# A new order of 1382 hand-ordered steps in a fused DeltaNet and feed-forward kernel

## The chip, the cores and the metric

The kernel runs on one core of one Trainium2 chip. The metric is the device time of one execution in microseconds (us). The engines have the profile's names: PE is TensorE (PEld is its loading of weights), DVE VectorE, ACT ScalarE, POOL GpSimd, and SP the engine that issues most of the DMA transfers.

## The reference

Inputs q, k, v have the shape 4 x 8 x 768 x 48 (batch, heads, tokens, features), beta 4 x 8 x 768. For each batch and head a state of 48 x 48 is carried over the tokens; the outputs of all heads side by side are a matrix x of 3072 x 384, which goes through a feed-forward block.

```python
k_n = k / (norm(k) + 1e-6)
for t in range(768):
    y[t] = q[t] @ state
    v_old = k_n[t] @ state
    state = state + beta[t] * outer(k_n[t], v[t] - v_old)
x = y as (3072, 384)                   # one row per token, heads side by side
out = (((x @ w1) * (x @ w2)) @ w3) @ w_out   # w1, w2: 384 x 1024, w3: 1024 x 1024, w_out: 1024 x 384
```

## The kernel before

The tokens are cut into 12 chunks of 64. Within a chunk the recurrence is solved as a whole: the scores of keys against keys form a strictly lower triangular matrix, its inverse is formed by elimination, and a few small products then give the outputs and the next state. Two chunks make a unit (512 tokens of all batches); each unit's outputs go through the feed-forward block, so there are six units, u = 0 to 5. The two last weights are multiplied once ahead (w3 @ w_out, the "fold"), after w3 has been transposed on PE.

Every part of the work is a Python generator, named by a letter and a number. `ORDER` (L39) is a text of 1382 names: `step` (L1320) advances the named generator to its next `yield`, which issues the instructions of one step, and `in_text_order` (L186) makes each engine keep the order in which its instructions were issued. Across engines only data and buffers order the work. The text is thus the queue of every engine, SP's and POOL's among them. The names:

- Loads on SP: k, q, v (chunks of the inputs), p (keys and queries of later chunks in another layout), P (pieces of the weights: load L838, a copy on ACT L846, a shift on DVE L851 and a sum on POOL L853 that rewrite the piece).
- K, Q (L369 on PE; 64 small products and copies on ACT L379 and DVE L381) and d (DVE) bring keys and queries into the layout of features. g and N make norms: squares on POOL (L301), sums on DVE (L303), and N's fifteen short operations on DVE.
- s (scores; s0 and s1 have 128 products at L409 and U on DVE at L420; the later ones L451, L457 with U and PT on DVE at L463, L474), h (scores of the first queries, L400, with PT on DVE at L434), u (U to memory, Ud, on SP).
- V (L497), one for each unit: the inverses by elimination. V0 takes U from on chip by a transpose on DVE (L505), V1 to V5 load Ub from Ud (SP, L510). Then 31 steps of two DVE operations each (L524, L529), each needing the one before. V0 and V1 eliminate in PSUM. V0 ends with four transposes on DVE (L533), the others with a store (SP, L549).
- e (L597): the corners that join two blocks of 32 into an inverse of 64: loads from Vd or, for e0 and e1, products on PE (L563); a transpose on DVE (T11, L602); products c1 and c2 on PE (L619) with copies on ACT.
- n scales v (POOL, L658). c (L664) is the chain from chunk to chunk: R, X and the state S, each one set of 64 products on PE (L672) and one DVE operation (L706, L717, L738). y (L744) gives the outputs: products on PE (L777), xT by ACT and SP.
- t (L900) transposes a part of w3, f (L910) folds: two halves of eight products (L913) and a copy on ACT.
- The feed-forward block: b (the first chunk of unit 0) and a0 to a4 are the products with w1 and w2 (`ab`, L927: six products at L934 and a copy on ACT, six more and a multiplication on DVE, L950), a50 to a53 those of unit 5 in another scheme (L1055). S, T, W and X are the sums on POOL and DVE that a Strassen-like scheme needs. o (L1143) is the product with the folded weight: seven steps of 16 products (L1166), and x (L1193) adds its parts (osb on ACT and DVE, L1197) and stores the result (SP).

PSUM is used as four banks (`ps_f`: a, b, t, f, o, K, Q, norms) and two pairs of banks (`ps_w`: scores, corners, chain, outputs, and V0 and V1 while they eliminate).

A step with large products lasts 2.6 us on PE (o, a, a half of f), a step with 64 or fewer small ones, of 32 to 64 columns, mostly less than 1 us. The order was written out in full; nothing in the file computes it.

Of the kernel before, what the change touches and what calls it, by code (L numbers as in the profile page):

```python
# [57 lines left out]
p5 c2 c2 e3 c2 x0 S0 o0 c3 S0 e3 c3 o0 e3 N2 y2 c3 x0 o0 d4 p5 y2 S0 c3 y3 x0 x0 x0 d5 d5 s4 s4
o0 x0 y3 s4 s4 d5 d5 s4 s4 N2 s5 y3 u4 s5 V2 s5 s5 s5 N2 s5 c3 u5 V2 x0 p6 x0 a14 p6 a14 a14 a14
a13 a13 V2 V2 V2 V2 V2 a12 a12 V2 a16 a16 V2 V2 V2 V2 V2 V2 V2 a15 V2 a15 a11 a11 V2 V2 V2 V2 V2  # L60
V2 V2 V2 V2 v5 x0 V2 a10 V2 V2 k6 V2 v4 V2 V2 V2 V2 a17 a17 a15 a15 a10 k7 d6 d6 d6 a10 a10 c3
S1 n5 n4 a13 a12 a12 a13 V2 e4 a17 e4 a11 g3 g3 g3 g3 a11 Q3 c4 g3 g3 n4 c4 e4 a16 a16 e5 e4 e4
e4 o1 x1 S1 a17 S1 S1 S1 e5 e5 S1 e5 d6 n5 g3 c4 c4 g3 o1 S1 c4 V3 c4 g3 e5 e5 o1 p7 g3 N3 c5 p7
# [6 lines left out]
S2 S2 d9 d9 p10 S2 e7 c7 S2 x2 o2 d9 d9 c7 S2 s8 c7 x2 s8 o2 s8 c7 S2 y7 S2 v8 n8 x2 K1 o2 x2 x2  # L70
u8 Q2 s9 s9 S2 S2 s9 y7 y7 s9 s9 u9 S2 o2 x2 s9 c7 x2 c7 V4 a32 a32 N4 k10 x2 x2 a36 a36 d10 d10
V4 a30 a30 V4 V4 a33 a35 Q1 V4 a37 V4 V4 V4 V4 a33 V4 V4 c8 V4 V4 V4 V4 a35 a37 V4 V4 V4 k11 a34
n9 a34 a31 p10 V4 V4 V4 V4 a34 V4 V4 V4 V4 x2 V4 V4 V4 V4 V4 V4 V4 e8 a31 d10 a31 a31 a35 a34 V5
a33 a30 a30 a36 n8 c8 K3 e8 e8 a35 a37 a33 a36 e8 K3 e8 e8 a37 a32 e9 e9 e9 p11 e9 c8 a32 o3 x3
S3 S3 g5 g5 g5 g5 n9 g5 S3 c8 d10 S3 S3 S3 c8 e9 p11 g5 g5 g5 o3 o3 e9 c8 c9 x3 x3 S3 S3 g5 g5
# [1283 lines left out]
```

## Time and profile before

| | before |
|---|---|
| time, median of 3 runs | 556.95 us (556.87 to 558.0) |
| the profiled execution: span | 556.1 us |
| its own time | not listed apart; the span is 0.85 us below the median of the runs |
| PE busy, instructions | 533.6 us (96%), 8732 |
| DVE busy, instructions | 343.7 us (62%), 800 |
| ACT busy | 145.7 us (26%) |
| POOL busy | 169.7 us (31%) |
| moved by DMA | 54.22 MB |
| instruction queue q8 | 68 packets, 1.11 MB |

By stages (start and end in us, PE busy, DVE busy, share of the DMA engines' time):

| stage | window | PE | DVE | DMA |
|---|---|---|---|---|
| loads, first scores | 0 to 32 | 20.41 | 23.40 | 0.92 |
| fold, V0, first chain | 32 to 100 | 66.58 | 51.04 | 0.82 |
| b and a0, V1 | 100 to 146 | 45.67 | 32.42 | 0.64 |
| o0 and the small steps of chunks 2 to 5 | 146 to 183 | 35.36 | 21.94 | 0.34 |
| a1, V2 | 183 to 227 | 44.00 | 32.04 | 0.61 |
| o1 and small steps | 227 to 265 | 36.27 | 22.58 | 0.47 |
| a2, V3 | 265 to 311 | 46.00 | 36.71 | 0.61 |
| o2 and small steps | 311 to 342 | 30.77 | 11.78 | 0.40 |
| a3, V4 | 342 to 388 | 46.00 | 32.26 | 0.44 |
| o3 and small steps | 388 to 420 | 31.59 | 17.86 | 0.26 |
| a4, V5 | 420 to 465 | 45.00 | 29.37 | 0.40 |
| o4 and small steps | 465 to 496 | 29.37 | 7.17 | 0.08 |
| a5 | 496 to 534 | 38.00 | 16.04 | 0.04 |
| o5, last results | 534 to 556.1 | 18.55 | 9.08 | 0.11 |

How to read it: the span is from the first to the last instruction of the profiled execution. Busy time of PE is counted from modelled ends of pipelined products. The granted clock of PE is 1.00 in every stage. A releaser named "issue" means that the engine waited for nothing that the profile shows.

### The profile page before, as it was taken

How to read it: one execution, taken by the hardware profiler on the slowest of the kernel's cores; microseconds unless marked ns; L12 is line 12 of the kernel's file. 1: busy time of each engine (PE TensorE's matmuls, PEld its weight loads, DVE VectorE, ACT ScalarE, POOL GpSimd, SP SyncE). 2: the span in 40 equal slices, each digit the busy share in tenths (PEclk: the TensorE clock that was granted, in tenths of full speed). 3: DMA queues.
4: the chain of work that ended last, by engine and by line, in shares of the span. 5: the costliest groups of instructions: out<-in, count | busy, mean ns of one | idle time of the engine just before them, and what ended most of it. 6: DMA issues, size and time to landing. Idle time of an engine off the chain costs nothing.

```text
span 556.1 us, 19932 instructions
## 1 busy us (share of the span) xinstructions
PE 533.6 (96%) x8732; PEld 390.8 (70%) x8732; DVE 343.7 (62%) x800; ACT 145.7 (26%) x291; POOL 169.7 (31%) x213
## 2 busy tenths in 40 slices
...
GB/s 189 339 307 230 158 140 150 128 160 55 96 48 55 119 147 72 67 88 89 122 74 100 70 91 80 126 38 83 51 15 154 26 60 38 18 58 1 0 2 57
DMA packets 191527, 54.22 MB, mean 98 GB/s; under 512 B 178928, under 2 KB 185072, under 8 KB 191440
## 3 DMA queue, kind: packets, MB, share of 16 engines
...
q8 instruction: 68, 1.11, 0.9%
...
## 4 chain that ended last, share of the span: by engine, by line
PE 93%; DVE 3%; issue 2%; DMA 2%; ACT 0%; SPq 0%; DVEq 0%
PE ps_f L934 38%; PE ps_f L1166 20%; PE ps_f L913 7%; PE ps_w L672 6%; PE ps_w L777 4%; PE ps_f L1074 4%; PE ps_w L619 3%; PE ps_w L1074 2%; PE ps_w L451 2%; PE ps_f L369 1%; PE ps_w L457 1%; PE ps_f L904 1%; DMA beta_fm<-in_beta_dram 1%; PE ps_w L409 1%; PE ps_w L1166 1%
## 5 line engine op out<-in xcount | busy, mean ns | idle before, releaser
L934 PE MATMUL ps_f<-xT,w2s 128*128 128x512 f32 (+1 forms) x288 | 106.9, 524 | 0.0
L934 PE MATMUL ps_f<-xT,w1s 128*128 128x512 f32 (+1 forms) x288 | 106.7, 524 | 0.0
L934 PEld LDWEIGHTS ps_f<-xT,w2s 128*128 128x128 f32 x288 | 54.1, 190 | 46.5 <-issue 41.6
L934 PEld LDWEIGHTS ps_f<-xT,w1s 128*128 128x128 f32 x288 | 54.0, 190 | 45.3 <-issue 41.6
L1007 POOL TENSOR_TENSOR ab<-ab 128x256 f32<-128x256 f32 x80 | 56.4, 731 | 78.7 <-DVE ab L950 73.8
L946 ACT COPY ab<-ps_f 128x512 f32<-128x512 f32 (+1 forms) x48 | 24.3, 515 | 134.4 <-PE ps_f L934 130.3
L1166 PE MATMUL ps_f<-w,ab 128*128 128x192 f32 x320 | 57.3, 332 | 1.9 <-DVE osb L1197 1.3
L1166 PEld LDWEIGHTS ps_f<-w,ab 128*128 128x128 f32 x320 | 51.6, 190 | 3.3 <-issue 2.4
L524 DVE TENSOR_TENSOR tb<-Vb,Ub 128x31 f32<-128x31 f32 (+15 forms) x124 | 43.0, 347 | 15.4 <-DMA Ub<-Ud 11.5
L529 DVE TENSOR_TENSOR Vb<-Vb,tb 128x31 f32<-128x31 f32 (+15 forms) x124 | 43.0, 346 | 4.3
L913 PE MATMUL ps_f<-wo,w3T 128*128 128x384 f32 x128 | 43.5, 491 | 0.4 <-ACT w3T L907 0.4
L1166 PE MATMUL ps_f<-room,ab 128*128 128x192 f32 x240 | 42.8, 332 | 0.0
L950 DVE TENSOR_TENSOR ab<-ab,ps_f 128x512 f32<-128x512 f32 (+1 forms) x48 | 27.4, 589 | 24.0 <-PE ps_f L934 24.0
L1166 PEld LDWEIGHTS ps_f<-room,ab 128*128 128x128 f32 x240 | 38.7, 190 | 0.7
L913 PEld LDWEIGHTS ps_f<-wo,w3T 128*128 128x128 f32 x128 | 23.5, 190 | 15.4 <-ACT w3T L907 0.5
L301 POOL TENSOR_TENSOR sq<-ktok 128x384 f32<-128x384 f32 x24 | 19.7, 835 | 43.5 <-DMA out_dram<-osb 16.9
L658 POOL TENSOR_TENSOR vtok<-vtok,n 128x384 f32<-128x384 f32 x24 | 19.8, 832 | 39.5 <-DMA vtok<-in_v_dram 39.5
L635 ACT COPY T<-ps_w 32x512 f32<-32x512 f32 x24 | 13.8, 577 | 67.2 <-PE ps_w L619 46.2
L795 ACT COPY xT<-ps_w 112x256 f32<-112x256 f32 x48 | 14.3, 384 | 65.0 <-PE ps_w L777 61.7
L451 PE MATMUL ps_w<-KQ 48*64 48x128 f32 x320 | 21.9, 274 | 1.8 <-DVE PT L474 1.5
L717 DVE TENSOR_TENSOR X<-ps_w,wt 128x768 f32<-128x768 f32 x12 | 11.5, 956 | 19.4 <-PE ps_w L672 12.9
L1197 DVE TENSOR_TENSOR room<-room,ps_f 128x384 f32<-128x384 f32 (+1 forms) x13 | 7.0, 537 | 26.4 <-PE ps_f L1166 26.4
...
## 6 DMA issues: line engine op xcount, KB each, us to landing
...
```

The source lines that it names most:

```text
L451: pe.matmul(ps[half(z), 0, n : n + 128], lhsT=x[:, 0, :], rhs=x.rearrange("p j t -> p (j t)"), start=True, stop=True,)
L524: dve.tensor_tensor(out=tv, in0=V[:, 0 : s + 1, s : s + 1].to_broadcast([P, s + 1, n]), in1=U[:, s, s + 1 : BS].unsqueeze(1).to_broadcast( ...
L529: dve.tensor_tensor(out=o, in0=o, in1=tv, op=ALU.subtract)
L672: pe.matmul(out(ps, r, h, z), lhsT=lhs(r, h, z), rhs=rhs(r, h, z), start=True, stop=True,)
L777: i = pe.matmul(region(h, z, r), lhsT=lhs, rhs=rhs, start=part[n] not in part[:n], stop=part[n] not in part[n + 1 :],)
L913: pe.matmul(ps[:, 0:DM], lhsT=w3Ts[jc, kc // 4][:, kc % 4 * P : kc % 4 * P + P], rhs=wo(kc), start=(kc == 0), stop=(kc == KF - 1),)
L934: pe.matmul(ps[:].rearrange("p b c t -> p b (c t)"), lhsT=w[:, m, js], rhs=x[:, m, :, c0:c1].rearrange("p b c t -> p b (c t)"), start=(m = ...
L946: act.copy(out=t, in_=ps)
L950: dve.tensor_tensor(out=t, in0=t, in1=ps, op=ALU.mult)
L1007: (dve if u == last else pool).tensor_tensor(out=o_, in0=x_, in1=y_, op=op)
L1074: pe.matmul(ps[:, j, :], lhsT=w[j], rhs=x, start=first and j == 0, stop=j == 1, skip_group_check=not first,)
L1166: pe.matmul(ps[b][:, b, :], lhsT=ab_of(u, HF * f + i, t0), rhs=ws_[w][:, i], start=first and i == 0 and (b == 0 or n == "F"), stop=i == HF ...
```

## The change

Only the text of `ORDER` is replaced, by another order of the same 1382 names; each name comes as often as before. So every engine does the same instructions, in a new order. In the new text runs of small steps on PE are shorter (at most five between two large ones, before up to seven), the 31 steps of an elimination mostly stand together, and the loads have other places in SP's queue. Cut to the lines that are spoken of (head and V0; e0 and the first chain; V1, b, a0 and o0; s6, s7 and o1; V3 and a2; a4 and o4; the end):

```diff
-k0 g0 g0 g0 K0 V0 g0 k1 P12 K0 K0 beta K1 P0 g0 g0 K1 K1 g0 q1 P12 g0 P12 P12 beta g0 g0 beta N0
-P8 P9 P8 P8 P8 P3 P0 P3 P3 P9 P0 s1 s1 s1 P9 s0 P3 P0 P13 P13 P13 s0 s0 V0 V0 V0 P1 P1 Q1 P1 P9
-Q1 P10 P13 V0 V0 Q1 P1 P10 P2 P2 t0 t0 P2 P4 P4 V0 t1 P2 t1 V0 P4 P4 h1 t4 t4 N0 P6 f0 P7 P10
-P10 P5 t2 t5 P18 V0 V0 P11 P6 V0 P6 P6 N0 P16 P19 V0 P7 P7 P5 P5 P5 q0 V0 t5 h1 P18 f2 P11 V0
...
-t9 v0 V0 P23 f4 f4 t14 f4 t15 t15 P21 P15 P15 t7 q3 V0 v1 Q2 Q2 V0 e0 h0 h0 e0 Q2 g1 e0 g1 t7 g1
-f3 e0 e0 K2 P27 K2 e1 e0 e0 n0 e1 k3 f7 P27 n0 e1 c0 e1 P21 e1 f7 V1 g1 c0 y0 P28 c0 P20 P25 f7
...
-s3 s3 s3 Q0 P30 P30 c1 b4 b4 P24 P24 u3 P24 y1 b5 b5 b5 V1 P26 y1 V1 b5 P31 V1 P32 b6 b6 P31 b4
-b0 b0 c1 b3 b4 b3 b7 V1 V1 b7 V1 V1 a02 V1 a02 V1 a03 V1 a05 V1 k4 V1 a00 V1 V1 P32 P32 a03 V1
...
-n3 V1 V1 b2 a00 a00 a05 a05 g2 g2 g2 g2 a06 n2 b1 b1 b0 e2 b0 a06 g2 b3 b3 b7 b7 o0 g2 c2 n3 x0
...
-x1 S1 x1 S1 y4 S1 y4 c5 o1 d7 d7 d7 d7 s7 s7 k8 g4 s7 s7 s6 s7 s7 u7 s6 s6 s6 s6 s6 c5 S1 c5 o1
-u6 y5 S1 x1 V3 o1 S1 x1 x1 c5 S1 y5 y5 S1 x1 V3 k9 S1 g4 c5 x1 x1 p8 V3 V3 V3 V3 V3 o1 c6 x1 V3
-V3 N3 N3 V3 V3 V3 V3 V3 V3 a27 a27 a25 x1 g4 a20 a25 a20 V3 V3 a25 a25 p8 a22 a22 V3 a24 a21 g4
...
-S5 o5 x4 Q2 x5 x5 x5 x5 x5 x5 x5 x5 x5 x5 x5 x5 K0 Q1
+V0 k0 K0 K0 g0 g0 k1 g0 g0 g0 g0 K0 K0 K0 K1 g0 g0 g0 beta beta P12 P12 P12 P12 P0 P0 P1 P1 P1
+P3 P3 beta g0 K1 P3 P3 P0 P0 P1 N0 P8 P8 P8 P8 s0 s0 K1 K1 K1 s0 t4 t4 P2 P2 P2 P2 q1 Q1 Q1 P9
+P9 P9 P9 s1 s1 s1 Q1 Q1 P4 P4 P4 P10 P10 P10 P10 P4 V0 V0 V0 V0 P13 P13 P13 P13 t1 V0 V0 V0 P5
+P6 t1 t0 t0 P6 P6 P6 P5 f2 P7 P7 t5 t5 V0 V0 P5 P5 V0 V0 f0 P7 P7 f2 P18 P18 P18 V0 V0 V0 V0
...
+Q2 V0 V0 P22 P22 t14 t15 P28 P29 t14 P28 P17 P17 t9 t9 t15 f4 f4 P29 P20 P20 f7 V0 V0 V0 V0 V0
+V0 V0 P28 P28 V0 V0 e0 e0 e0 h0 h0 e0 e0 f4 k2 g1 K2 K2 e1 e1 K2 e0 e0 f3 g1 g1 e1 e1 e1 n0 n0
...
+b4 b4 P34 b7 b7 s3 P32 b4 b6 b6 b4 u2 u3 P31 y1 V1 V1 V1 V1 V1 V1 g2 P25 a02 V1 P32 V1 V1 P31 T
+T P32 p4 V1 V1 V1 V1 V1 V1 V1 V1 a02 b0 b2 b2 a06 b0 a06 a00 a05 b3 b3 a00 a03 a03 a07 a05 a01
+b1 b1 a01 a07 V1 V1 V1 V1 V1 a03 a03 a00 a00 b5 a04 a04 v3 p4 b5 V1 V1 V1 c2 N1 N1 b1 b1 V1 V1
+V1 V1 V1 a02 a02 b0 b0 V1 V1 V1 V1 b3 b3 g2 n2 c2 V1 a01 a01 k5 g2 a04 a04 b7 b7 a07 a07 a06
+a06 d4 b2 b2 a05 a05 n3 n3 T T o0 V1 V1 e2 e2 e2 e2 d4 d4 d4 g2 o0 g2 g2 g2 e2 x0 o0 v4 e3 e3
...
+c5 c5 o1 v6 n6 s6 s6 s6 s6 s6 s6 s7 s7 s7 s7 s7 s7 u7 u6 x1 k8 o1 x1 c5 c5 o1 x1 x1 x1 x1 V3 y5
+y5 y5 c5 c5 n6 S1 S1 S1 o1 c6 V3 V3 V3 k9 N3 x1 x1 x1 a23 a23 N3 V3 V3 V3 V3 V3 V3 V3 V3 V3 V3
+V3 V3 V3 V3 d8 V3 a22 a27 a20 a20 g4 V3 V3 V3 V3 V3 g4 a25 a22 a22 a27 a22 V3 g4 g4 g4 g4 d8 g4
+V3 V3 V3 V3 V3 a20 a20 a25 a25 p8 V3 V3 V3 e6 a25 a24 a26 a26 d8 e6 d8 a26 a24 a26 a24 a21 a21
...
+V4 V4 V4 V4 V4 V4 V4 V4 V4 V4 V4 V4 V4 V4 V4 a34 a34 a37 a37 c7 a31 a31 a36 a30 a30 a35 a35 a36
...
+o5 S5 S5 o5 S5 S5 x5 o5 S5 o5 o5 x5 x5 o5 S5 o5 x5 x5 x5 x5 x5 x5 x5 x5 x5 x5 x5 K3 K3 Q0 Q1
```

A name such as a02 is slab 2 of unit 0, a50 the first scheme of unit 5; a name that is listed after its generator has ended does nothing (the last K, Q).

More of the change, by code (lines that the diff above doesn't have):

```diff
@@ L58 @@
[L58 to L63, printed above, removed]
@@ L70 @@
[L70 to L75, printed above, removed]
@@ new lines @@
+P3 P3 beta g0 K1 P3 P3 P0 P0 P1 N0 P8 P8 P8 P8 s0 s0 K1 K1 K1 s0 t4 t4 P2 P2 P2 P2 q1 Q1 Q1 P9
+P9 P9 P9 s1 s1 s1 Q1 Q1 P4 P4 P4 P10 P10 P10 P10 P4 V0 V0 V0 V0 P13 P13 P13 P13 t1 V0 V0 V0 P5
+P6 t1 t0 t0 P6 P6 P6 P5 f2 P7 P7 t5 t5 V0 V0 P5 P5 V0 V0 f0 P7 P7 f2 P18 P18 P18 V0 V0 V0 V0
+P19 P11 P11 V0 P11 P19 f2 f0 f0 P18 t10 t10 t2 t2 P23 q0 Q0 Q0 Q0 Q0 V0 P19 P19 V0 V0 V0 N0 h1
+h1 V0 V0 N0 P14 P16 P16 V0 t11 t11 f5 P11 t3 P23 P23 P16 P23 P15 P15 P14 v0 P22 P22 P17 V0 V0
+V0 f5 f5 P17 t3 f1 f1 P16 t8 t8 f1 P21 P14 P14 t6 t6 P15 P15 h1 t7 t7 V0 P21 h0 q2 Q2 Q2 Q2 Q2
@@ new lines @@
+Q2 V0 V0 P22 P22 t14 t15 P28 P29 t14 P28 P17 P17 t9 t9 t15 f4 f4 P29 P20 P20 f7 V0 V0 V0 V0 V0
+V0 V0 P28 P28 V0 V0 e0 e0 e0 h0 h0 e0 e0 f4 k2 g1 K2 K2 e1 e1 K2 e0 e0 f3 g1 g1 e1 e1 e1 n0 n0
+c0 P29 P29 P20 P20 P30 P30 P30 P30 f7 f7 K2 K2 P35 P35 P21 c0 c0 c0 f3 f3 P35 P35 g1 k3 K3 y0
+y0 K3 K3 t12 g1 g1 g1 P21 c1 q3 t12 P33 P33 P33 t13 t13 P25 P27 P27 f6 g1 P24 g1 v1 n1 n1 c1 e1
+e1 Q3 Q3 Q3 Q3 Q3 P26 P26 s2 c1 g1 f6 f6 P27 P27 P33 N1 P26 V1 P26 s2 s2 s2 P31 P31 v2 n2 c1 y1
+y1 s2 s2 s3 s3 P25 P25 s3 k4 g2 y0 y0 b6 b6 g2 P32 P24 P24 P24 s3 s3 P34 c1 P34 b5 b5 P34 c1 y1
```

47 lines of the change are left out of this document (24 added, 23 removed).

## The prediction

> **What bounds the kernel now.** I read the busy shares first, then the chain that ended last.
>
> ```profile
> span 556.1 us, 19932 instructions
> PE 533.6 (96%) x8732; PEld 390.8 (70%) x8732; DVE 343.7 (62%) x800; ACT 145.7 (26%) x291; POOL 169.7 (31%) x213
> ...
> q8 instruction: 68, 1.11, 0.9%
> ...
> PE 93%; DVE 3%; issue 2%; DMA 2%; ACT 0%; SPq 0%; DVEq 0%
> ```
>
> PE bounds it: busy 533.6 of 556.1 us and 93% of the chain. An order that removes nothing can only win idle PE time (22.5 us), and of that the 2% "issue" and 3% DVE of the chain are the part an order reaches. "Issue" comes from one source. The timeline's chain (start, us), two windows that begin at 0 (us; then busy and count for PE, PEld, DVE, ACT, POOL; clock; DMA share; GB/s) and the PE waits show it.
>
> ```profile
> 13.95 0.95 issue
> 16.96 4.42 issue
> 0.00:14.50 14.50, 8.62 (x220) 7.16 (x221) 9.19 (x23) 3.59 (x5) 9.99 (x22) 1.00 0.98 198
> 0.00:21.30 21.30, 10.67 (x348) 8.97 (x349) 13.76 (x37) 8.63 (x15) 13.13 (x25) 1.00 0.97 256
> 0.00:98.10 98.10, 85.22 (x1874) 60.80 (x1875) 73.45 (x172) 62.46 (x117) 50.70 (x60) 1.00 0.85 216
> 0.00:102.55 102.55, 89.24 (x2000) 63.97 (x2001) 75.21 (x175) 64.84 (x124) 52.59 (x61) 1.00 0.86 214
> 98.13 0.27 PE L777 MATMUL ps_w<-KQ,S 48*48 48x64 f32 x3 [0.53 <-issue]
> 168.80 1.02 PE L672 MATMUL ps_w<-R,TT 64*64 64x48 f32 x54 [0.45 <-issue]
> 251.84 0.32 PE L672 MATMUL ps_w<-R,TT 64*64 64x48 f32 x5 [0.33 <-issue]
> ```
>
> Add PE and PEld: 441, 697, 3749 and 4001 instructions stood ahead of four such waits. 697−441 = 256; 4001−3749 = 252, and the few semaphore instructions that no record counts fill the rest; 3749−697 = 3052 is 12×256 less 20. So these waits fall on every 256th instruction, and queue q8 brought 68 packets of 1.11 MB / 68 = 16 KB: PE waits for its own next block of code. It runs dry where many short instructions follow each other. The body's waits of this kind (0.3 to 0.5 us in the rows, with the slow start behind each one) come to an estimated 2.1 us; the head's largest is 4.42.
>
> The rest of the idle time is in these stages (head; second slab; chains of the first and second unit; the fifth's), and these steps wait in them:
>
> ```profile
> 0.00:32.00 32.00, 20.41 (x558) 16.48 (x559) 23.40 (x64) 18.58 (x36) 20.58 (x32) 1.00 0.92 271
> 146.00:183.00 37.00, 35.36 (x1133) 32.70 (x1135) 21.94 (x46) 8.01 (x18) 10.14 (x15) 1.00 0.34 56
> 227.00:265.00 38.00, 36.27 (x1128) 33.40 (x1116) 22.58 (x53) 6.86 (x16) 13.12 (x19) 1.00 0.47 85
> 465.00:496.00 31.00, 29.37 (x789) 27.22 (x779) 7.17 (x12) 6.85 (x16) 12.15 (x18) 1.00 0.08 21
> 181.18 0.33 PE L451 MATMUL ps_w<-KQ 48*64 48x128 f32 x2 [0.42 <-DVE PT L474]
> 247.81 0.33 PE L451 MATMUL ps_w<-KQ 48*64 48x128 f32 x2 [0.46 <-DVE PT L474]
> 493.45 2.84 PE L1166 MATMUL ps_f<-w,ab 128*128 128x192 f32 x16 [1.32 <-DVE osb L1197]
> ```
>
> **The change part by part.** I give every PE step the shortest spacing to its successor that the same kind has in this trace, and call the excess a wait. A wait by that measure is longer than the idle in a row (it holds the slow start after it): 2.5 us in o0's stage, where 1.64 is idle. The floors of all 331 steps sum to 520.1 in the old order.
>
> Keeping small apart from large costs something of its own. A large step runs longer beside small ones:
>
> ```profile
> 420.25 15.61 PE L934 MATMUL ps_f<-xT,w1s 128*128 128x512 f32 x36
> 461.80 2.84 PE L934 MATMUL ps_f<-xT,w2s 128*128 128x512 f32 x6
> ```
>
> 36 products in 15.61 us are 2.60 per step; 2.84 between two small ones, about 0.1 per border. The old text has 55 groups of small steps (20 singles, 22 pairs, 13 of three to seven), the new 56 (15, 29, 12, none over five). One group more and its borders: +0.3 (520.4).
>
> The head. Its loads and first scores decide when inverse V0 starts, and V0 is a DVE chain which e0 waits for:
>
> ```profile
> 22.48 1.29 DVE L420 TENSOR_TENSOR U<-ps_w,wt 128x512 f32<-128x512 f32 x2 [0.42 <-PE ps_w L409]
> 23.80 2.04 DVE L505 STREAM_TRANSPOSE Ub<-U 128x1024 f32<-128x1024 f32 x1
> 40.03 0.60 PE L904 MATMUL ps_f<-ident,w 128*128 128x128 f32 x4
> 62.72 1.29 DVE L434 TENSOR_TENSOR PT<-ps_w,smask 128x512 f32<-128x512 f32 x2
> 63.93 0.70 DVE L602 STREAM_TRANSPOSE T<-TT 128x512 f32<-128x512 f32 x1
> 28.77 0.41 DVE L851 TENSOR_SCALAR w<-w 128x512 uint32<-128x512 uint32 x1
> 23.18 1.28 POOL L853 TENSOR_TENSOR w<-w,raw 128x512 uint32<-128x512 uint32 x1
> 32.29 7.91 PE L913 MATMUL ps_f<-wo,w3T 128*128 128x384 f32 x24
> ```
>
> The new text puts t4 and Q1 ahead of s1, so instruction 705, the block border, falls inside s1. If the block arrives at 21.4 as now (16.96+4.42), s1 ends near 23.5, its two U's near 24.9 (now 23.8). On SP, q1's four loads move behind P0, P1, P3, P8 and P2, landing near 19.4 by the pace of loads now; Q1 is a product and so still fits the wait. V0's transpose (2.04) then ends at 26.9, P13's shift (0.41) and its sum on POOL (1.28) follow, which with the copies queued there puts t5 near 30 and f0 behind it. With f2, f0 and the t's between, the step that is at 40.03 now comes at 40.4: +0.4. Bounds: −1.6 (block 1.5 earlier, since large steps now stand ahead of it) to +2.4 (block and q1 each a load later).
>
> V0 and e0. The chain is 62.7−23.8 = 38.9 now. From 24.9 it would end at 63.8; h0.1 and h0.2 still follow it, two weight shifts fewer stand in it (−2×0.41), but P6, P22, P17 and P28 are queued in it right behind their loads, in a stretch where DMA is 0.92 busy; I add 2.7 (bounds 0 and 4) and have 65.7. PE needs, from the t10 that starts at 38.7, 7 halves of folds (18.2; 7.91 for three), 10 transposes (4.7), Q0, Q2, h1, h0 (4.0): 26.9, so e0.0 at 65.9 with 0.3 of waits. The race is even. Then a new wait: e0's first c1 product (L619) follows e0.0 at once and needs the two banks that h0 filled, and DVE does e0.2 (0.70) and h0.1, h0.2 (1.29) first: 0.5+0.7+1.3 less the short step, 1.7. Now Q2, g1 and others stand between. Further to b6.0: a state sum behind four weight shifts 0.65, f6 behind t12's copy 0.4, s2 behind N1's fifteen short operations 0.4. Total 3.35 against 3.2 by the same measure now: +0.15.
>
> First slab (b, a0). With b6.0 at 100.4: c1.4 waits 0.4, a02 for xT's transfer 0.5, a block 0.2, a bank 0.4, against 0.8 now: +0.7.
>
> V1, between them on DVE:
>
> ```profile
> 113.21 0.19 DVE L524 TENSOR_TENSOR tb<-ps_w,Ub 128x31 f32<-128x31 f32 x1 [1.61 <-DMA Ub<-Ud]
> 137.48 0.20 DVE L529 TENSOR_TENSOR ps_w<-ps_w,tb 128x31 f32<-128x31 f32 x1
> 138.87 0.34 SPq L549 DMA_DIRECT2D Vd<-Vb  x1
> 147.55 0.71 DVE L602 STREAM_TRANSPOSE T<-TT 128x512 f32<-128x512 f32 x1
> ```
>
> On SP its load of Ub (V1.1) now stands behind P32, P34, u2, u3 and y1.3, whose inputs are there before it; u3's store, which needs the last scores of s3, sets it, as now, so I leave the start at 113.2 (0 to +1 for the two weight loads ahead). 31 steps run from 113.2 to 137.7 with 9 other operations between; the new text puts 11, and two of them multiply a bank that PE has not filled when DVE comes to them (b1, b0), +2.0: end 139.7. From there the copy, the store, eight loads and T11 take 10.1 (147.55−137.48): e2.1 at 149.5 to 150, c1 after it at 150.3. PE reaches c1 (e2.2) at 100.4 + 47.5 (37 steps: 32 half-width products and five more) + 0.7 = 148.6. A wait of 1.4 to 1.8 that isn't there now: +1.4.
>
> o0's stage. s4 and s5, c3 and y2, y3 now alternate with o0's steps: s5 0.5, c3 0.45, y3 0.15 = 1.1 against 2.5: −1.4.
>
> a1, V2, o1. a17's second half and e4.1 come just in time: 0. In o1's stage s6 and s7 still follow each other as four small steps and wait for PT twice, 0.5+0.45 = 1.0, against 3.0 (1.73 of it idle): −2.0. If only idle time can be won, the two stages give −2.4 and not −3.4.
>
> a2 and V3. Its start hangs on Ub's load, for which V2 gives the price:
>
> ```profile
> 188.13 0.34 SPq L510 DMA_DIRECT2D Ub<-Ud  x1
> 192.96 0.19 DVE L524 TENSOR_TENSOR tb<-Vb,Ub 128x31 f32<-128x31 f32 x1 [3.51 <-DMA Ub<-Ud]
> ...
> L524 DVE TENSOR_TENSOR tb<-Vb,Ub 128x31 f32<-128x31 f32 (+15 forms) x124 | 43.0, 347 | 15.4 <-DMA Ub<-Ud 11.5
> ```
>
> 192.96−188.13 = 4.8. In the new text SP reaches V3.1 behind x1's result (1.2 after o1.5's end) and two stores (0.6). Then 4.8, 29 steps at 2×0.347 plus gaps 22.3 (L529 costs the same as L524), nine other operations 5.05: 33.9 from o1.5's end. PE runs 32.8 to a26.2 (floors of 16 steps 35.5 less o1.5's own 2.7), which needs the bank of a20.3, queued behind V3.30: 1.1 wait, none now: +1.1.
>
> o2, o3, o4: −0.5 (fewer blocks run dry); o4.6 keeps its wait of 1.32 for x4. Tail: 0, same last steps.
>
> Moved and costed at nothing:
>
> ```profile
> L1007 POOL TENSOR_TENSOR ab<-ab 128x256 f32<-128x256 f32 x80 | 56.4, 731 | 78.7 <-DVE ab L950 73.8
> ...
> 100.00:146.00 46.00, 45.67 (x383) 39.77 (x375) 32.42 (x90) 14.61 (x34) 24.12 (x26) 1.00 0.64 112
> ```
>
> The slab sums S, the scalings n and the sums W on POOL (31% busy; if o caught up with its S, each late one would cost 0.73); the loads k, v and p on SP after 100 us, where DMA is 0.64 busy or less and each stands a stage ahead of its use; V4 and V5, now one block of steps on DVE, behind eight first products each of a3 and a4 whose results ACT takes: 8×2.60 = 21 us against about 22 for the steps, so that, uncovered, each costs 1 to 2.
>
> Sum: +0.3 +0.4 +0.15 +0.7 +1.4 −1.4 −2.0 +1.1 −0.5 = +0.15. The profiled execution spans 556.1, 0.85 under the median of 556.95 (556.87 to 558.0). The forecast is 556.95+0.15 = 557.1.
>
> The body's "issue" waits. By count of the PE work per 320 instructions (256 and the 64 already fetched), the old order falls to 2.9 us at two places and below 3.8 at four; the new one stays above 4.3 outside the head. The o0 and o1 terms hold this 2.1 us gain. The Trainium skill, page "Runtime: NRT & Kernel Launch", section "Instruction fetch mechanics", says that instructions come in 16 KiB blocks of 256 by a DMA queue of their own, which the 68 packets confirm, and that a crossing is mostly hidden; the 4.42 and 0.53 us waits speak against that here. By that rule the 2.1 us would not be won and the time would be 559.2.
>
> **Rivals.** *The DVE chains finish ahead of PE*: V0 without 2.7 of load waits ends at 63, V1 without its two bank waits at 137.7, V3 with cheaper neighbours. Then 1.7, 1.4 (+0.4) and 1.3 vanish: −4.8, 552.3. For it: DVE is 62% busy only; the bounds of each chain allow it. Against: V0's loads, which DMA's 0.92 makes real.
>
> *V0 is late*, the slower side. e0.0 and all that follows moves one for one once V0 ends after 65.9. If the block or q1 arrives 3 us later than I put it (t4 and Q1 ahead of s1 give one more load to wait for), V0 starts at 28 and the time is 557.1+3 = 560.1. It decides from a start of V0's transpose above about 25.1. Refill hidden (559.2) belongs to this side.
>
> *The order does nothing*: waits move from one place to the next one for one, as PE's queue is full either way: 557, too.
>
> **How the numbers follow.** My forecast .42, 555.0 to 559.0 by V0's 1.6 either way and V1's and V3's 1 each. Faster rival .31. Late V0 .19, hidden refill .03. No effect .05. 0.2% of 556.95 is 1.1 us, about what a measurement of this kernel can tell from no change: faster is below 555.8, slower above 558.1. From the forecast .05 faster, .28 same, .09 slower: faster .05+.31 = .36, same .28+.05 = .33, slower .09+.22 = .31. The range 552.0 to 560.5 takes in both rivals' own times and leaves their outer ends, about 2 in 10.
>
> **What would show it.** PE's clock at 1.00 throughout. V0's transpose (L505) at 24.9; e0's first transposed corner (L602) at 65 to 66, an L619 wait of 1 to 2 us behind it. "Issue" waits after 100 us at none or below 0.3. V1's last L529 near 139.5 and an L619 wait near 149. Waits on PT (L474) in the stages of o0 and o1 halved. The wait for osb at o4 again. Wrong if V0 starts after 25.1, if V1 ends before 138, or if a new wait stands where I put none: a1 (e4) and a3 (e8) have about 1 us of spare.

## The result and the profile after

The new order takes 574.44 us (573.79 to 581.1, four runs), beside 557.09 for the old one on the same chip: a ratio of 1.0336, 95% interval 1.0284 to 1.0388. It is 3.4% slower; the forecast was 557.1, the top of the range 560.5. The profiled execution spans 572.1 us, 16.0 more than the old one's 556.1. All times are medians of runs in the fast state; one run each of k8_later and old_head fell in the slow one and does not count.

The first parts of the page of after: span, busy time (share, instructions), the instruction queue, and the chain that ended last.

```profile
span 572.1 us, 19901 instructions
PE 538.3 (94%) x8732; PEld 392.5 (69%) x8732; DVE 352.8 (62%) x800; ACT 144.7 (25%) x291; POOL 170.2 (30%) x213
...
q8 instruction: 68, 1.11, 0.8%
...
PE 72%; issue 8%; DMA 8%; DVE 5%; SPq 3%; ACT 2%; POOL 1%; ACTq 0%; POOLq 0%; DVEq 0%
```

The work is the same (8732 products, 68 blocks of code). The chain is not: PE's share fell from 93% to 72%, and "issue" (8%), DMA (8%) and SP's queue (3%, 0% before) took its place. The share of "issue" must not be read as waits of PE. Most of it is one piece, which belongs to POOL: it stood idle ahead of a square (of the keys that k6 loads) while PE worked on.

```profile
174.27 36.49 issue
210.99 0.84 POOL sq L301
```

With the same products PE's busy time grew by 4.7 us and its idle time by 11.3. The ten largest PE waits of after (waited for, total us, times, longest us):

```profile
PE ps_f L369 <- DMA ktok<-in_k_dram: 5.1, 3, 4.1
PE ps_f L934 <- DMA xT<-xT: 3.9, 1, 3.9
PE ps_f L369 <- ACT spare L849: 2.8, 1, 2.8
PE ps_f L904 <- issue: 1.9, 1, 1.9
PE ps_f L904 <- POOL w L853: 1.9, 1, 1.9
PE ps_f L934 <- DVE ab L950: 1.7, 1, 1.7
PE ps_f L913 <- ACT w3T L907: 1.5, 1, 1.5
PE ps_f L1166 <- DVE osb L1197: 1.3, 1, 1.3
PE ps_f L913 <- issue: 1.1, 1, 1.1
PE ps_w L619 <- DVE T L602: 1.0, 1, 1.0
```

The first and the eighth stand in the old order too (4.3 and 1.3). Where the 16 us arise shows in the starts of the same steps in both traces (us):

| step | old | new | later by | between this row and the one above |
|---|---|---|---|---|
| e0, first c1 product | 66.36 | 69.82 | 3.46 | head, fold, V0: +3.5 |
| b6 | 100.11 | 106.16 | 6.05 | first chain: +2.6 |
| o0, first step | 145.68 | 151.66 | 5.98 | b, a0, V1: −0.1 |
| o0, last step | 175.75 | 182.05 | 6.30 | o0: +0.3 |
| o1, first step | 227.41 | 236.99 | 9.58 | s4, s5, a1, V2: +3.3 |
| o1, last step | 261.36 | 269.18 | 7.82 | o1: −1.8 |
| e6, c1 | 301.53 | 315.03 | 13.50 | a2, V3: +5.7 |
| o2, last step | 338.86 | 352.67 | 13.81 | o2: +0.3 |
| o3, last step | 417.55 | 432.65 | 15.10 | a3, V4, o3: +1.3 |
| o4, last step | 493.45 | 508.88 | 15.43 | a4, o4: +0.3 |
| o5, last step | 549.79 | 565.21 | 15.42 | a5, o5: 0 |

At each of these starts PE has the same products behind it in both orders, but for one exchanged step and a few small ones of the norms. One stage is better in the new order (o1), and four hold nearly all of the loss: the head with the fold, the first chain, a1 and a2.

**PE's clock in the head.** Four rows of PE's timeline of after, then one of before:

```profile
25.98 1.97 PE L904 MATMUL ps_f<-ident,w 128*128 128x128 f32 x8 [1.85 <-POOL w L853]
27.73 4.58 PE L913 MATMUL ps_f<-wo,w3T 128*128 128x384 f32 x8
40.33 1.04 PE L904 MATMUL ps_f<-ident,w 128*128 128x128 f32 x8
44.02 2.75 PE L913 MATMUL ps_f<-wo,w3T 128*128 128x384 f32 x8
```
```profile
24.25 1.47 PE L904 MATMUL ps_f<-ident,w 128*128 128x128 f32 x8
```

Eight transposes take 1.97 us at 25.98 and 1.04 at 40.33, eight products of the fold 4.58 at 27.73 and 2.75 at 44.02. So PE ran at about half speed up to some 31 us (in the old order the spacing of the eight at 24.25 falls from 213 to 110 ns at 25 us), although the profile gives its clock as 1.00 there. That 1.00 is no measurement: the trace's record of the granted clock begins at 31.42 us (in the old order at 25.07), and the profile counts a time without a record as 1.00. The trace of phase120 (below) has a record of the head, with 0.50 from 17.01 to 34.07 us, and there the same eight transposes take 1.97 as well. The 1.00 of the first stage of the old order is of this kind too. From 25.98 us on PE worked without a gap but for f1's wait of 1.47. The slow clock cost it 0.93 + 1.83 = 2.8 us there, against 0.4 in the old order, and so accounts for 2.3 of the 3.46 us by e0, unless PE had waited for its inputs instead. Why the clock came up 6 us later is not shown.

**Waits for code.** The head's waits of this kind nearly went (5.4 us to 0.3), but those of the body grew: the rows of 0.2 us or more come to 1.6 us in the old trace and to 5.6 in the new one. In PE's timeline of after:

```profile
90.27 0.27 PE L904 MATMUL ps_f<-ident,w 128*128 128x128 f32 x1 [1.91 <-issue]
95.39 0.38 PE L369 MATMUL ps_f<-ident,X 64*48 64x64 f32 x11 [0.50 <-issue]
179.88 0.56 PE L777 MATMUL ps_w<-KQ,S 48*48 48x64 f32 x25 [0.99 <-issue]
184.32 1.79 PE L1166 MATMUL ps_f<-w,ab 128*128 128x192 f32 x10 [1.03 <-issue]
```

and the windows from 0 to just before three waits (columns as in the prediction's windows), with the ten us around the first:

```profile
0.00:90.25 90.25, 75.39 (x1491) 53.37 (x1492) 65.71 (x146) 56.69 (x107) 48.91 (x57) 1.00 0.91 231
0.00:95.37 95.37, 80.00 (x1618) 56.41 (x1618) 68.62 (x153) 59.58 (x112) 50.15 (x58) 1.00 0.91 226
0.00:99.65 99.65, 83.14 (x1746) 58.87 (x1746) 72.49 (x166) 61.83 (x116) 52.55 (x61) 1.00 0.89 220
82.00:92.00 10.00, 7.95 (x212) 5.71 (x211) 4.76 (x9) 5.18 (x13) 5.72 (x6) 1.00 0.99 204
```

2983, 3236 and 3492 instructions (PE and PEld) stand ahead of them: 253 and 256 apart, so three blocks in a row came late, one of them in the middle of a fold step (99.67, 1.15 us in the chain), a large step with small ones around it. Counted with the semaphore and drain instructions of PE's queue, which the windows leave out, 449 + 256k instructions stand ahead of every wait for code of 0.2 us or more in all traces of this case. In the last row the DMA is 0.99 busy; in the same ten us of the old trace it was 0.55.

**Loads in SP's queue.** a23 waited 3.90 us for xT, and PE's clock fell behind that wait. SP's queue and PE in the timeline of after, then three windows of it, then SP's queue of before:

```profile
266.90 3.34 SPq L233 DMA_DIRECT2D ktok<-in_k_dram  x4
270.34 0.57 SPq L1182 DMA_DIRECT2D out_dram<-osb  x1
271.01 0.41 SPq L510 DMA_DIRECT2D Ub<-Ud  x1
271.47 4.34 SPq L806 DMA_DIRECT2D xT<-xT  x6
277.11 8.37 PE L934 MATMUL ps_f<-xT,w1s 128*128 128x512 f32 x15 [3.90 <-DMA xT<-xT]
```
```profile
274.00:276.00 2.00, 0.00 (x0) 0.00 (x0) 0.00 (x0) 0.00 (x0) 0.00 (x0) 1.00 0.66 227
276.00:278.00 2.00, 0.89 (x1) 0.44 (x2) 1.56 (x7) 0.00 (x0) 0.00 (x0) 0.79 0.34 70
278.00:280.00 2.00, 2.00 (x4) 0.94 (x3) 1.83 (x9) 0.00 (x0) 0.00 (x0) 0.50 0.77 132
```
```profile
241.26 3.14 SPq L233 DMA_DIRECT2D ktok<-in_k_dram  x4
256.23 0.34 SPq L510 DMA_DIRECT2D Ub<-Ud  x1
258.51 4.22 SPq L806 DMA_DIRECT2D xT<-xT  x6
```

In the new order k8's four transfers, 3.34 us of issuing, stand ahead of V3's Ub and of xT; in the old one SP issues them at 241.26, when it has nothing else. The granted clock is 0.50 from 277.18 to 280.59 us, and a23's product step took 4.34 us instead of 2.68. The Trainium skill ("TensorE: Matmul & The Clock Gate", "HAM oscillation — how this bites in real kernels") gives idle gaps of PE over about 3.4 us as the bound from which the clock goes to half; the 3.90 us here agree. The 2.24 us that k8_later (below) waited for code at 88.31 do not: its clock was 0.50 from 88.01 to 91.42.

The same shape, once each, in a1 and in o3's stage:

```profile
211.84 0.55 DVE L303 TENSOR_REDUCE ss<-sq 128x8 f32<-128x384 f32 x1 [1.78 <-POOL sq L301]
224.59 1.99 PE L934 MATMUL ps_f<-xT,w2s 128*128 128x512 f32 x4 [1.69 <-DVE ab L950]
400.56 0.55 DVE L303 TENSOR_REDUCE ss<-sq 128x8 f32<-128x384 f32 x1 [5.11 <-POOL sq L301]
401.03 0.70 DVE L602 STREAM_TRANSPOSE T<-TT 128x512 f32<-128x512 f32 x1
401.79 0.77 PE L619 MATMUL ps_w<-T,U 33*33 33x32 f32 x64 [1.04 <-DVE T L602]
```

A sum of g3 stands in DVE's queue among V2's steps and waits for POOL's square, and that for a load (k6) behind p6's sixteen transfers; V2 ends 1.8 us later and a12 waits 1.7 for its bank. At 400 us a sum of g5 waits for k11, and e9's transpose stands behind it.

### The profile page after: what moved, and what is told of

Read it like the earlier page. It is cut to its first block, busy times and chain, and to the rows that moved or that the text cites. A ratio compares the mean times of both kernels' runs of the same rounds, so it can differ in the third digit from the quotient of the medians.

```text
span 572.1 us, 19901 instructions
## 1 busy us (share of the span) xinstructions
PE 538.3 (94%) x8732; PEld 392.5 (69%) x8732; DVE 352.8 (62%) x800; ACT 144.7 (25%) x291; POOL 170.2 (30%) x213
## 4 chain that ended last, share of the span: by engine, by line
PE 72%; issue 8%; DMA 8%; DVE 5%; SPq 3%; ACT 2%; POOL 1%; ACTq 0%; POOLq 0%; DVEq 0%
PE ps_f L934 30%; PE ps_f L1166 16%; PE ps_w L672 5%; PE ps_f L1074 4%; PE ps_f L913 4%; DMA X<-in_q_dram 3%; PE ps_w L777 3%; PE ps_w L619 2%; PE ps_w L1074 2%; DMA raw<-in_moe_w_dram 2%; DMA ktok<-in_k_dram 1%; PE ps_w L451 1%; PE ps_w L457 1%; DMA raw<-in_moe_w_out_dram 1%; SPq L491 1%
## 5 line engine op out<-in xcount | busy, mean ns | idle before, releaser
L524 DVE TENSOR_TENSOR tb<-Vb,Ub 128x31 f32<-128x31 f32 (+15 forms) x124 | 44.4, 358 | 26.0 <-DMA Ub<-Ud 22.2
L913 PE MATMUL ps_f<-wo,w3T 128*128 128x384 f32 x128 | 45.8, 508 | 2.6 <-ACT w3T L907 1.5
L706 DVE TENSOR_TENSOR R<-vtok,ps_w 128x768 f32<-128x768 f32 x11 | 10.4, 946 | 23.3 <-POOL vtok L658 14.0
L524 DVE TENSOR_TENSOR tb<-ps_w,Ub 128x31 f32<-128x31 f32 (+15 forms) x62 | 21.1, 340 | 3.2 <-DMA Ub<-Ud 1.5
L529 DVE TENSOR_TENSOR ps_w<-ps_w,tb 128x31 f32<-128x31 f32 (+15 forms) x62 | 21.7, 349 | 2.1
```

Of the source, the lines that this page charges most:

```text
L524: dve.tensor_tensor(out=tv, in0=V[:, 0 : s + 1, s : s + 1].to_broadcast([P, s + 1, n]), in1=U[:, s, s + 1 : BS].unsqueeze(1).to_broadcast( ...
L529: dve.tensor_tensor(out=o, in0=o, in1=tv, op=ALU.subtract)
L913: pe.matmul(ps[:, 0:DM], lhsT=w3Ts[jc, kc // 4][:, kc % 4 * P : kc % 4 * P + P], rhs=wo(kc), start=(kc == 0), stop=(kc == KF - 1),)
```

## Experiments

Each is timed beside the old order on the same chip; ratios are to it. A kernel that takes part of one order and the rest of the other has its names in the first order up to the cut, then those that are left in the other order.

**Where the loss arises: half of each order.**

```diff
-(the old order)
+(new_head: the new order up to the first b6, what is left in the old order)
+(old_head: the old order up to the first b6, what is left in the new order)
+(new_to_e0: the new order up to the first e0, what is left in the old order)
```

> The new order up to the first step of b6 (the end of head, V0 and first chain), what is left then in the old order. Theory (the lateness is a sum of local waits, one for one from where they stand): b6 began at 106.16 us in the new trace and at 100.11 in the old, so the time is that of before plus 6.0 (5 to 7.5): 563. Rival (the late head makes every later chain late, and the body's waits follow from it): plus 12 to 16, 569 to 573.

> The old order up to b6, what is left then in the new order. Theory (local waits add up): the whole 16 less the head's 6, before plus 9.9 (8.5 to 11): 567. In the trace the wait of a23 for xT (3.9 us) and of a12 (1.7 us) stand as in the new order. Rival (the body's waits follow from the late head): before plus 0 to 3, 557 to 560.

> The new order up to the first step of e0 only (loads, fold, V0), then the old order. Theory (the 6 us by b6 are two separate things: 3.5 us by e0's first c1 product from later weights, and 2.6 us after it from waits for code): before plus 3.5 (2.5 to 4.5), 560.5, and between e0 and b6 the waits of the old order. Rival (all of it comes from the head, the rest follows): plus 4.5 to 6, as much as the run with the new order up to b6.

new_head: 561.04 us, 1.0078 (1.0048 to 1.0108), beside 556.89; in its trace b6 starts 5.4 us later than in the old order's and the last step of o5 5.45. The lateness of the head stays what it is through 450 us of old order: local and one for one, as the theory has it. The median is 4.2 us over the old order's, a little under the 5 to 7.5 that were expected. new_to_e0: 563.18, 1.0107 (1.0089 to 1.0124), beside 557.18. e0's c1 product is 4.27 later, b6 5.3 and the end 5.43: that misses the theory's 3.5, but the step after the cut has a wait that neither order has (2.8 us at 76.42, for a copy of e0's corner on ACT, with the clock at 0.50 for 6.8 us from 74.90), so the split between fold and first chain is not settled by this run. old_head: 578.23, 1.036 (1.0311 to 1.0409), where 567 was expected. Here too the cut made a wait of its own:

```profile
112.01 1.95 SPq L806 DMA_DIRECT2D xT<-xT  x3
114.06 4.30 SPq L491 DMA_DIRECT2D Ud<-U  x8
118.41 1.87 SPq L806 DMA_DIRECT2D xT<-xT  x3
120.38 4.18 PE L934 MATMUL ps_f<-xT,w1s 128*128 128x256 f32 x9 [6.84 <-DMA xT<-xT]
```

a02 waits 6.84 us because u2's and u3's stores stand between the two halves of xT. Taking out that wait and the 2.4 us of slow clock behind it, 9.3, leaves 569, 12 over the old order and not "0 to 3" as the rival had it. After that cut the trace waits 1.3 at a12 and 3.1 at a23, where the clock costs 1.6 more: these waits stand behind the old head too. This run alone does not part the order from lateness, as its own wait had made the body 12 us late; new_head does, with 5.4 us of lateness and none of these waits.

**Do the waits for code hang on the count of instructions?** 64, then 120 calls of a tiny product ahead of the first step, nothing else:

```diff
     for _ in range(4):
-        bank([P, 512])
+        ps0 = bank([P, 512])
     for _ in range(2):
         two_banks()
+    [pe.matmul(ps0[0:16, 0:16], lhsT=ident[0:16, 0:16], rhs=ident[0:16, 0:16], start=True, stop=True) for _ in range(64)]
```

> The new order, with 64 tiny products (16x16) added on PE before the first step, in time in which PE waits for the first keys. They add 128 instructions, half a block of 256, and nothing else. Theory (PE waits for code at the borders of blocks, each 256th instruction, and what a border costs depends on which steps stand just ahead of it): every border moves by half a block against the steps, the six issue waits of the body (5.8 us in all) leave their places, and others come at recorded instruction 449+256k of the new count; worked out from the measured starts of PE's instructions with a fetch that begins 1.5 to 2 us after its trigger, 8 to 18 us more than the new order: 582 to 592. Rival (these waits belong to the places in the order, for example to the transposes and scores themselves): the same six waits at the same steps, 574 to 575.

> The new order with 120 tiny products ahead instead of 64: 240 instructions, so that each border of a block falls 16 instructions earlier in the work than in the new order (256-240). Theory (block borders): the same working gives no body wait or under 1 us in all, so 4 to 6 us won there; the products last up to 1 us longer than PE's first wait for keys, and the head's own borders move too (plus or minus 3): 567 to 573. Rival (waits belong to places): 574 to 576.

576.47 us (1.0349, 1.0311 to 1.0387) and 579.74 (1.0414, 1.0352 to 1.0476); both intervals overlap the new order's. Neither made the shift that was planned. The pages count 8860 and 8972 products instead of 8732: each call became two products, each with its load of weights, so 256 and 480 instructions were added and not 128 and 240. That is a whole block for phase64, whose borders fall on the same steps as the new order's, and two blocks less 32 for phase120, whose borders fall 32 instructions later in the work and not 16 earlier. So the 8 to 18 us more and the 4 to 6 less were not tested. The waits for code of phase64's body:

```profile
86.18 0.99 PE L777 MATMUL ps_w<-PT,X 64*48 64x64 f32 x54 [0.73 <-issue]
100.86 1.77 PE L913 MATMUL ps_f<-wo,w3T 128*128 128x384 f32 x5 [0.52 <-issue]
184.78 1.57 PE L1166 MATMUL ps_f<-w,ab 128*128 128x192 f32 x8 [0.45 <-issue]
```

The last two stand at the steps of the new order's waits at 99.67 and 184.32; the first is a block ahead of that at 90.27, where now no wait of 0.2 us is left. With the borders on the same steps the body's waits came to 1.7 us instead of 5.6, so the steps ahead of a border do not set what it costs. That the place is a matter of the count alone rests on the rule 449 + 256k above, which holds in both traces. phase120's clock of 0.50 in the head is no loss against the new order, which ran at half speed there as well.

**Does the DMA's load delay the code?** The old order with 16 copies of 512 KB in o3's stage, each ahead of a PE step:

```diff
+    def extra():
+        for n in range(16):
+            x = dram.tile([P, 2 * CW], U32, tag=f"extra{n}", name=f"extra{n}", bufs=1)
+            act.dma_start(out=x[:], in_=moe_w3[0:P, 0:CW].bitcast(U32))
+            yield
+    parts["D"] = extra
-... o3 x3 S3 S3 ... c8 ... e9 ...
+... D o3 x3 S3 S3 ... D c8 ... D e9 ...
```

> The old order, with 16 copies of 512 KB each from memory to memory added in the stage of o3 (about 388 to 418 us), on ACT's queue; nothing reads them. In this stage the DMA is 0.26 busy, there are small steps as in the other stages, and no wait for code over 0.1 us. Theory (a block of code comes over the same DMA engines as the data, so it comes later where they are busy, and that is why the waits for code stand where loads are dense): the fetches in this stage begin 1 to 3 us later after their trigger, waits for code of 0.3 to 1.5 us come at recorded instructions 449+256k, 2 to 6 us in all, 559 to 563. Rival (the fetch has a way of its own, the waits come from the number of small instructions alone): no wait for code in this stage, 557 to 558 (ACT's issues).

572.19 us, 1.0276 (1.0248 to 1.0303). The waits in PE's timeline and two windows of its trace:

```profile
404.57 0.88 PE L777 MATMUL ps_w<-PT,X 64*48 64x64 f32 x19 [5.18 <-issue]
412.37 0.97 PE L1166 MATMUL ps_f<-w,ab 128*128 128x192 f32 x5 [1.03 <-issue]
421.96 1.31 PE L777 MATMUL ps_w<-PT,X 64*48 64x64 f32 x37 [4.05 <-issue]
```
```profile
395.00:400.00 5.00, 4.39 (x158) 4.02 (x157) 1.03 (x2) 0.48 (x1) 1.44 (x3) 1.00 0.97 229
405.00:410.00 5.00, 4.92 (x116) 4.62 (x109) 1.49 (x5) 1.19 (x4) 0.00 (x0) 0.50 0.99 237
```

The same steps in the same order, which waited for no code with the DMA 0.26 busy, waited 5.18, 1.03 and 4.05 us with it 0.97 to 0.99 busy, and the clock fell to 0.50 on top. The three blocks' own transfers (q8) began when PE had 0, 10 and 0 instructions left before the border, in the old trace 295, 75 and 239. The theory holds, with more than its 2 to 6 us: code comes late where the DMA is loaded. This load is not the only way to a wait, as the old order's 0.45 us at 168.80 stand in a stretch (165 to 169 us) with the DMA 0.02 busy. And the load here is higher than in most of the first chain; that its 2.6 us come from the loads is argued from the two traces, and no run took loads out of it.

**The loads' places in SP's queue.**

```diff
 k8_later, one move:
-... u7 u6 x1 k8 o1 ... V3 y5 y5 y5 c5 ...
+... u7 u6 x1 o1 ... V3 y5 y5 y5 k8 c5 ...
 queue3: k8_later, and k6 ahead of p6, e9's loads ahead of k11, e9's transpose ahead of g5's second sum
 q1_earlier, one move:
-... beta P12 ... P0 P0 P1 ... P2 q1 Q1 ...
+... beta P12 ... P0 P0 q1 P1 ... P2 Q1 ...
 queue4: queue3 and q1_earlier
```

> The new order with one step moved: the load k8 goes behind y5's transfers of xT on SP's queue, where it stood ahead of them. Theory (a load that stands on SP ahead of a transfer on the path costs its issue time, 3.3 us): a23's wait for xT falls from 3.9 us to about 0.5, PE's clock does not fall to half behind it (1.7 us), 5.1 us less than the new order: 569.3. Rival (PE would meet the next late thing, V3 or a bank, and the wait moves on): 0 to 2 less, 572 to 574.

> The new order with one step moved: q1's load goes back to its old place on SP, behind P0 and ahead of P1. Theory (the head is late because Q1 stands ahead of s1 on PE and its load behind five pieces of weights): Q1's wait of 3.2 us and 0.8 behind it go, V0 starts 3 us earlier, and 2.5 to 3.5 us are won: 571. Rival (the head is bound by the DMA, 0.97 busy: the pieces of weights come later by as much, and t1, f0 and f1 wait instead): 0 to 1 won, 573.5 to 574.5.

> As k8_later, and two places more of the same kind: k6 goes ahead of p6 on SP (the squares of g3 wait for it, and V2's steps wait on DVE behind their sum), and e9's loads go ahead of k11, with e9's transpose ahead of g5's sum that waits for k11 on DVE. Theory (places in SP's queue): a12's wait of 1.7 us for a bank and e9's of 1.1 go as well, 8.0 less than the new order: 566.4. Rival (waits move on): 570 or more.

> The moves of queue3 and q1_earlier together. Theory (places in SP's queue explain most of the 16 us and add up): 11 less than the new order, 563.4 (562 to 566); what is left are the waits for code between 85 and 110 us and about 180 us (some 4 us more than in the old order) and the first pieces of weights. Rival: 568 or more.

k8_later: 569.55 us, 1.0215 (1.019 to 1.024): 5.0 us less than the new order (17.35 over its old order, now 12.39), as the theory has it. In the traces the stretch from o1's last step to e6 takes 41.6 us instead of 45.9 (old order: 40.2). Timeline of PE and a window:

```profile
272.24 13.14 PE L934 MATMUL ps_f<-xT,w1s 128*128 128x512 f32 x30 [1.28 <-DMA xT<-xT]
```
```profile
275.00:280.00 5.00, 5.00 (x13) 2.21 (x12) 4.59 (x13) 0.59 (x1) 0.00 (x0) 1.00 0.85 186
```

The wait is 1.28 instead of 3.90 and the clock stays at 1.00. q1_earlier: 574.93, 1.0308 (1.0278 to 1.0337), no gain, as the rival had it. Q1's wait fell from 2.77 us to 0.83, and t1's wait for a piece of w3 from POOL rose from 1.85:

```profile
28.18 1.97 PE L904 MATMUL ps_f<-ident,w 128*128 128x128 f32 x8 [4.55 <-POOL w L853]
```

One wait went and another came, so the order of these loads chose only who waits. V0 did not start earlier (28.60 against 26.40), and the clock's record begins at 31.90, as late as in the new order: what an earlier V0 or an earlier clock is worth, this run does not show. queue3 and queue4: 570.08 (1.0244, 1.0215 to 1.0273) and 569.98 (1.0233, 1.0196 to 1.0269), where 566.4 and 563.4 were expected: the moves did not add up. In both, e9's transpose overwrites T11, which has one buffer, before e8's second products, which so read chunk 9's corner; and e9's part of their question stays unanswered by them.

**All three loads ahead of what they block, and v0.**

```diff
 queue5: k8 behind y5, k6 ahead of p6, k11 behind e9's loads, three g5 steps behind e9's transpose
 queue6:
-... p6 p6 V2 V2 k6 ...            p8 c5 ... k8 ... y5 y5 y5
+... k6 p6 p6 V2 V2 ...            k8 c5 ... ... y5 y5 y5 p8
-V4 (31 steps) V4 ... c7 ... c7 ... e8 ... k11
+c7 c7 V4 (31 steps) k11 V4 ... e8 ...
 queue6_v0: queue6, and v0 behind k2
```

> The new order with k8 behind y5's transfers, k6 ahead of p6, and k11 behind e9's loads with g5's squares and sums of chunk 11 behind e9's transpose. Theory (places in SP's queue): a23's wait (with the clock's fall) 5.1, a12's 1.7 and e9's 1.1 less than the new order, 7.9: 566.5. Rival (waits move on): 570.

> The new order with k6 ahead of p6, k8 in p8's place and p8 behind y5's transfers, and k11 ahead of V4's store, for which the last products of c7 (they free k11's buffer) go ahead of V4's steps. Theory (the loads stand in SP's queue where they block a transfer on the path or come too late for the squares behind which V's steps queue on DVE): the lateness against the old order no longer grows from a1 to o3: a12's wait (1.7 us), a23's with the clock (5.6) and e9's (1.1) go, 8.4 less than the new order, 566. Rival (the long runs of steps make a2 and a3 late whatever the loads do): 569 or more.

> As queue6, and v0's load goes back behind k2, so that P22, P17 and P21 come before it. Theory (f1's second half waits for a transposed piece whose load stands behind v0): its wait of 1.5 us goes and e0 starts 1.5 earlier, 564.5. Rival (the head is bound by the sum of loads): as queue6.

queue5: 571.38 us, 1.0256 (1.0214 to 1.0298), no better than k8_later alone. e9's wait is gone (e8's and e9's c1 are both 10.15 later than in the old order), but o3's last step is 15.47 later: a load put behind the transfers comes late for its own squares, and the wait came back at o3. queue6: 569.79, 1.0213 (1.0181 to 1.0245); queue6_v0: 568.61, 1.0199 (1.017 to 1.0229), 6.1 us less than the new order (17.35 now 11.25), where 8.4 and 10 were expected. All three intervals overlap that of k8_later, so no gain beyond k8's is shown. a12's wait, 1.69 us in the new order, was 1.32 in queue6 and gone in queue5 and queue6_v0; e9's is gone in all three. But queue6_v0's a1 still loses 1.1 and its a2 1.8 us (from the last step of o0 to the first of o1, and from the last of o1 to e6), and from o2's last step to e8, where the new order lost nothing, it loses 2.0 now that c7 stands ahead of V4.

Nor is v0's part shown. f1's wait is gone in queue6_v0 and e0's c1 comes at 68.05, but in k8_later and queue5, where v0 has the new order's place, f1's wait is gone too, and e0's c1 comes at 67.46 and 67.28 (new order 69.82). In the eleven traces that have the new order up to b6, or nearly so (q1 or v0 moved, small products ahead), e0's c1 lies between 67.28 and 71.71 and b6 between 104.68 and 107.41; the earliest e0 has its b6 at 105.47, so little of an earlier e0 arrives. What sets b6 stays open. Places in SP's queue are thus shown for about 5 of the 17 us (k8); moving k6 and k11 took waits of PE away, but no time that the runs can tell.

**Can the better stage be had alone?**

```diff
 old_with_new_o1: the old order, from d7 to V3's first step in the new one's order, k8 behind y5
 o1_step_before_c5:
-... s6 s6 s6 s6 s6 c5 S1 c5 o1
+... s6 s6 s6 s6 s6 o1 c5 S1 c5
 o1_step_before_s6:
-... s7 s7 s6 s7 s7 u7 s6 s6 s6 s6 s6 c5 S1 c5 o1
+... s7 s7 o1 s6 s7 s7 u7 s6 s6 s6 s6 s6 c5 S1 c5
```

> The old order with the steps from d7 to V3's first elimination step in the new one's order (s6 ahead of s7, an o1 step between s7 and c5), and k8 behind y5's transfers. Theory (the one stage in which the new order is better is o1's, by 1.7 us from o1.0 to o1.6, of which the wait for code at 251.84, the scores' and the chain's waits are a part): 0.7 to 1.7 us less than before, 555.3 to 556.2. Rival (that gain depends on where blocks of code and the earlier steps fall): 0, 557.

> The old order with one step moved: o1's fifth step goes ahead of c5's second set of products (L672) on PE. Theory (in the old order five small steps stand there in a row, and PE waits 0.4 us for c5's input and 0.7 behind it, a block of code among it; a large step ahead of them covers both): 0.7 to 1.3 less than before, 555.6 to 556.3. Rival: 0, 557.

> The old order with one step moved: o1's fifth step goes between s7 and s6. Theory (the scores wait for PT, 0.7 and 0.3 us, because two pairs of banks serve four sets of scores in a row; a large step gives DVE the time): these and the wait of c5 go, 1.0 to 1.7 less, 555.2 to 556; against it u6's store and V3 come 1.5 us later, and if a26 had no spare they are lost again: 557.

old_with_new_o1: 568.13 us, 1.0211 (1.0184 to 1.0239). o1's last step is 1.42 us earlier than in the old order, the gain that was expected; then a2 loses it and 11 us more by e6, since g4's square waits for k8, which now stands last, V3's steps and a store's osb queue behind the sum on DVE (6.83 us idle), PE waits 2.61 for xT and 5.72 for the bank, and its clock falls to 0.50 twice. The single moves: 558.41 (1.0021, 1.0007 to 1.0034) and 557.97 (1.0013, 0.9999 to 1.0028), beside 557.36. Neither wins; the second takes the scores' first wait and finds others of its size. No version here beats the old order.

## Why the prediction was wrong

**The sum.** It gave +0.15 and the trace has +16.0. By its terms, against the table of starts:

- Groups of small steps, +0.3: the floors of both orders stand as counted; nothing in the runs speaks against it.
- The head, +0.4, and V0 up to e0, a part of +0.15: measured +3.5 by e0's first c1. The working gives t10 (the step at 40.03 in the old order) two times, 40.4 at the end of the head and 38.7 ahead of e0. The trace has 40.33, and e0.0's 65.9 was added up from 38.7; from 40.33 the same 26.9 and 0.3 give 67.5. It came at 69.25, with f1's wait of 1.47 on top. The mechanism was wrong too. No block of code held up s1, which the working had waiting until 21.4; Q1's load did that. V0's transpose started at 26.40 (24.9 forecast), for the reason that was the slower rival's: Q1 ahead of s1, and its load behind five pieces. But the price was not V0's. V0's chain took 40.5 us (40.8 worked out) and was done at 66.85, ahead of PE, so the race was not even and the wait of 1.7 behind e0 did not come. PE was late by itself, most of it by the half speed up to 31 us. The working had put the clock at 1.00 throughout, which for the head rests on rows without a record of it.
- V0 to b6, what is left of +0.15 (whose listed waits behind e0 come to 3.15, not 3.35): measured +2.6 behind e0, as much as the waits for code grew there (0.9 to 3.6). The step that failed is "the new one stays above 4.3 outside the head" and with it the claim that the o0 and o1 terms hold a gain of 2.1. I took the time that a fetch needs as a constant of about 4 us and counted PE's work against it. The fetch is not constant: extra_dma_o3 made it several us longer with load alone, and phase64 has 1.7 us of waits where the new order, with its borders on the same steps, has 5.6. The loads are denser where the first of the new waits stand (0.99 against 0.55 from 82 to 92 us).
- b and a0, +0.7, and V1, +1.4: measured −0.1. V1's chain took 26.3 us, as worked out (26.5), and PE came to e2 as late as b6 made it; the corner behind V1 took 7.5 us and not the 10.1 that I took from the old trace as a whole. The corner was mis-sized by 2.6.
- o0, −1.4, measured +0.3 over o0's own steps (with a wait for code of 0.99 at 179.88). o1, −2.0, measured −1.8: the size was right; how much of it the scores' and the chain's waits are, and how much the code at 251.84, was not parted.
- a1, 0, measured +3.3 with s4, s5 (of it 1.0 for code at 184.32 and 1.7 at a12); a2, +1.1, measured +5.7 (of it 3.9 for xT and 1.7 by the clock; V3's own wait of 1.1 did not come); a3 and o3, part of −0.5, measured +1.3 (e9's 1.0). The waits at a12, a23 and e9 are one step of the working, the one that cost most: "the loads k, v and p on SP after 100 us … each stands a stage ahead of its use", costed at nothing. k6, k8 and k11 did not. I looked at when their data are used and not at what stands behind them: on SP, where four transfers take 3.3 us to issue, and on DVE, where a sum that waits for the load holds up V's steps or a corner. For k8 the runs show the price, some 5 us.

**The rivals.** "The DVE chains finish ahead of PE" came true for V0 and V1 and won nothing, as PE was later than either. "V0 is late" had the sign and neither the size nor the cause. That the refill of code is hidden did not come out: the 2.1 us were indeed not won, but since more code came late in the body, not less. The 3.9 us wait brought a fall of the clock, which no term had.

**The signs set out.** V1's length, the osb wait at o4 (1.3) and fewer waits for PT (1.5 us in four to 1.0 in two) came as listed, and so did one sign of being wrong, V0's start after 25.1. "Issue" waits after 100 us at none, the waits of L619 behind e0 and near 149, and the clock at 1.00 throughout did not. Still open: why PE's clock came up later in the head, what sets b6, and why queue6_v0's a1, a2 and a3 still lose 5 us; 0.6 us after o5's last step was not looked into.
